# Joins of two 32-blocks at once on 64 rows, a schedule that counts instructions in lots of 256, and the fourth unit inverted in larger blocks on the vector engine

## The chip, the cores and the metric

One core of one Trainium2 chip. The time is the device time of one launch in microseconds (us); a run is one execution, and a kernel is judged by the median of its runs and by its ratio to the kernel before on the same chip.

## The reference, cut to what matters

```python
# deltanet: q, k, v of (4, 8, 768, 48), beta of (4, 8, 768)
for t in range(S):                       # 768 steps
    y[:, :, t] = einsum('bhd,bhde->bhe', q[:, :, t], state)
    v_old = einsum('bhde,bhd->bhe', state, k_n[:, :, t])
    state = state + beta * einsum('bhd,bhe->bhde', k_n[:, :, t], v[:, :, t] - v_old)
# mixer on x = y as (4, 768, 384)
u = x + (x^T U V)^T
out = u + relu(u @ w_ch1) @ w_ch2
```

The kernel turns the 768 steps into 12 chunks of 64. Each chunk and head needs the inverse of a 64x64 unit triangular matrix. A "unit" is half a batch: 6 chunks of all 8 heads. There are eight units. A batch's recurrence needs its two units inverted; its mixer then gives TensorE 288 large matmul passes (128x128 by 384 columns, `p_f` and `p_o`; a *pass* is one matmul instruction as the profile counts it, and a call in the program makes two: the 384 calls of `p_e` are 768 passes in the kernel before), which also fill TensorE's gaps in other batches' stages.

## The kernel before

Inversion starts on VectorE on small diagonal blocks: the 48 heads and chunks of a unit have two diagonal blocks of 32x32 each, 96 blocks on 96 partitions. Units 0 to 3 do this in 16x16 blocks (`split = 2`, 15 steps of two VectorE instructions). Two *joins* on TensorE then make 32x32 and 64x64 inverses of them. Units 4 to 7 do it in 32x32 blocks (`split = 1`, 31 steps), and only the second join is left. Joins run in thirds of a unit. The first join, `p_e` and `p_d`, is what the change rewrites:

```python
split = 2 if n < 4 else 1                # n: the unit
...
quarter = [slice(BK * i, BK * i + BK) for i in range(4)]      # BK = 32
p_e = ps_of([128, TQ, SB], "p_e")                             # TQ = 8, SB = 16
for e, (c, j, r) in enumerate(where):                         # 8 slots of two heads and chunks
    for i, rows in enumerate(quarter):                        # four calls each
        at = slice(BK * (i % 2), BK * (i % 2) + BK)
        nc.tensor.matmul(p_e[rows, e], pg[rows, c, j, r, at], zc[rows, e, SB:BK], ...)
...
turned(zn, zc)                                                # VectorE transposes
nc.scalar.mul(xe, p_e, mask_e)
...
for e in range(TQ):
    for rows in quarter:
        nc.tensor.matmul(p_d[rows, e], zn[rows, e], xe[rows, e], ...)
```

A small scheduler in the kernel's Python orders all work. Each `step(pe=, dve=, act=, ...)` gives an estimated duration per engine, and the work that could start first is emitted next. Each engine's queue is filled in that order.

The first stage of a unit runs thus: Gram matrices `pg` to memory (`scr`), back as `gs`, then ScalarE takes the keys' norms from its diagonal (`nc.scalar.sqrt(norm, gs...)`), then VectorE inverts.

## Time and profile before

| | before |
|---|---|
| time, 4 runs | 673.27 us median (671.5 to 675.08) |
| span of the profiled run | 672.2 us |
| first pass of `p_e`; last but one right side of the first batch made | 41.73; 112.6 us |
| first batch's front (`p_tt`), first large pass `p_f` | 120.6; 130.47 us |
| unit 2's joins | 152.14 to 179.12 us |
| last pass of TensorE | 668.8 us |

A *right side* is the VectorE subtraction `rhs` with which each chunk of the recurrence begins (eleven of a batch). The *front* is the mixer's start, which waits for the recurrence's end. The profile's lines are shown in the prediction.

### The profile page before, as it was taken

Reading aid. Unit: us, or ns where it says so; the run is one execution under the profiler, and the core shown is the slowest. Engines: PE = TensorE matmul, PEld = TensorE weight load, DVE = VectorE, ACT = ScalarE, POOL = GpSimd, SP = SyncE. Lnnn points to the kernel's source line nnn. Section 1 sums busy time; section 2 is a strip of 40 time slices with the busy share of each in tenths; the row PEclk is TensorE's granted clock in tenths of the full one; section 3 lists DMA queues with packets and bytes.
Section 4 is the critical chain, followed back from the end, with each engine's and each line's share of the span. In section 5 each row is a group of like instructions: output and inputs, shape, how many; then the busy total and the mean of one; then the engine's idle time right before and its main releaser. Section 6 shows DMA issues by size and latency. Waiting matters only on the chain.

```text
span 672.2 us, 21750 instructions
## 1 busy us (share of the span) xinstructions
PE 619.1 (92%) x9696; PEld 391.7 (58%) x9696; DVE 302.2 (45%) x739; ACT 189.4 (28%) x479; POOL 227.3 (34%) x378
## 2 busy tenths in 40 slices
PE   4468877897998999999998999999999999999997
PEld 3357766555655665555655555566565555555554
DVE  3498656994472122895861106869811112100000
ACT  3314645334501553102211331133113310310210
POOL 9653185856260393824501825530000000000000
PEclk9655555896899699999998999999999999999999
DMA  8766266665132133316212323251030000000000
GB/s 130 187 150 159 69 155 166 153 168 111 40 94 51 38 74 80 77 39 139 39 45 57 88 41 73 61 112 32 14 72 14 2 14 13 12 1 23 12 13 23
DMA packets 83566, 47.73 MB, mean 71 GB/s; under 512 B 71984, under 2 KB 76640, under 8 KB 83472
## 3 DMA queue, kind: packets, MB, share of 16 engines
q0 software_dynamic: 14528, 26.98, 17.0%
q1 hardware_dynamic: 64208, 18.66, 12.6%
q8 instruction: 76, 1.25, 0.8%
q10 hardware_dynamic: 4736, 0.69, 0.6%
q14 instruction: 18, 0.15, 0.1%
HBM read 35.29 MB, written 11.01 MB: 69 GB/s over the span
## 4 chain that ended last, share of the span: by engine, by line
PE 87%; DVE 4%; DMA 3%; issue 3%; ACT 2%; SPq 0%; ACTq 0%; DVEq 0%
PE p_f L1057 31%; PE p_o L1078 29%; PE p_y L889 5%; PE p_g L542 4%; PE p_s L923 3%; PE p_s L937 3%; PE p_y L945 2%; PE p_d L824 2%; PE p_x L844 2%; PE p_v L861 1%; PE p_e L811 1%; PE p_u L1021 1%; PE p_h L1011 1%; PE p_tt L987 1%; DVE xt L691 1%
## 5 line engine op out<-in xcount | busy, mean ns | idle before, releaser
L1057 PE MATMUL p_f<-ut,w_sb 128*128 128x384 f32 x576 | 213.3, 515 | 0.0
L1078 PE MATMUL p_o<-w_sb,h_f 128*128 128x384 f32 x576 | 203.1, 497 | 0.0
L1057 PEld LDWEIGHTS p_f<-ut,w_sb 128*128 128x128 f32 x576 | 107.1, 196 | 65.0 <-issue 3.9
L1078 PEld LDWEIGHTS p_o<-w_sb,h_f 128*128 128x128 f32 x576 | 104.2, 189 | 63.9 <-issue 1.2
L1039 ACT ACTIVATE h_f<-p_f 128x384 f32<-128x384 f32 x96 | 47.1, 491 | 159.0 <-PE p_f L1057 158.9
L475 POOL DMA_DIRECT2D qn<-in_k_dram x96 | 58.7, 619 | 52.8 <-DVE qt L484 43.3
L414 POOL DMA_DIRECT2D vn<-in_v_dram x64 | 41.9, 666 | 88.8 <-DVE rhs L916 81.5
L475 POOL DMA_DIRECT2D qn<-in_q_dram x96 | 58.8, 620 | 22.2 <-DVE prod L685 14.4
L1044 DVE TENSOR_TENSOR x<-x,p_o 128x384 f32<-128x384 f32 x24 | 13.2, 553 | 112.5 <-PE p_o L1078 112.3
L691 DVE TENSOR_TENSOR xt<-xt,prod 96x30 f32<-96x30 f32 (+20 forms) x184 | 56.9, 309 | 6.3
L685 DVE TENSOR_TENSOR prod<-gs,xt 96x30 f32<-96x30 f32 (+20 forms) x184 | 56.4, 306 | 5.0
L960 DVE TENSOR_TENSOR s<-s,p_s 128x192 f32<-128x192 f32 x40 | 14.1, 352 | 92.1 <-PE p_s L937 81.2
L967 ACT COPY x<-p_y 64x192 f32<-64x192 f32 x96 | 30.1, 314 | 53.8 <-PE p_y L945 50.1
L916 DVE TENSOR_TENSOR rhs<-vn,p_y 128x192 f32<-128x192 f32 x44 | 15.6, 354 | 65.4 <-PE p_y L889 64.9
L932 ACT COPY z<-p_s 128x192 f32<-128x192 f32 x48 | 15.3, 319 | 103.7 <-PE p_s L923 103.4
L414 POOL DMA_DIRECT2D kn<-in_k_dram x48 | 31.4, 663 | 6.7 <-PE p_s L937 5.8
L923 PEld LDWEIGHTS p_s<-rhs,zt 64*64 64x64 f32 x704 | 17.2, 158 | 25.9 <-issue 19.3
L923 PE MATMUL p_s<-rhs,zt 64*64 64x48 f32 x704 | 23.0, 254 | 6.5 <-DVE rhs L916 4.9
L889 PEld LDWEIGHTS p_y<-s,kt 48*64 48x64 f32 x704 | 16.7, 155 | 18.8 <-issue 10.3
L937 PEld LDWEIGHTS p_s<-z,kn 64*64 64x64 f32 x704 | 16.8, 155 | 17.2 <-issue 12.5
L945 PE MATMUL p_y<-z,qk 64*64 64x48 f32 x768 | 23.1, 242 | 0.5 <-ACT z L932 0.5
L889 PE MATMUL p_y<-s,kt 48*64 48x48 f32 x704 | 22.5, 250 | 1.0 <-ACT x L967 1.0
(132 smaller groups left out, 622.3 us busy)
## 6 DMA issues: line engine op xcount, KB each, us to landing
wide<-in_moe_w_ch_dram POOLq DMA_DIRECT2D x7, 768.0 KB, 5.6
vn<-in_v_dram POOLq DMA_DIRECT2D x64, 72.0 KB, 2.6
out_dram<-x SPq DMA_DIRECT2D x24, 192.0 KB
kn<-in_k_dram POOLq DMA_DIRECT2D x48, 72.0 KB, 2.5
gs<-scr SPq DMA_DIRECT2D x8, 384.0 KB
scr<-xt SPq DMA_DIRECT2D x8, 384.0 KB
scr<-pg SPq DMA_DIRECT2D x30, 96.0 KB
stage<-in_moe_w_ch_dram POOLq DMA_DIRECT2D x3, 768.0 KB, 5.1
```

The costliest lines, as they stand in the source:

```text
L414: engines[queue].dma_start(out=t[half(g ^ (s % 2) if crossed else g), :, s], in_=src[b, 4 * g + s, hf * UC * L : (hf + 1) * UC * L, :].rea ...
L475: nc.gpsimd.dma_start(out=places[rows, x, j, :, 0 : ds.stop - ds.start], in_=src[b, h, hf * UC * L : (hf + 1) * UC * L, ds].rearrange("(m ...
L685: nc.vector.tensor_tensor(out=prod, in0=gb[:, :, j : j + 1, j + 1 :].to_broadcast([NP, split, m, w]), in1=xb[:, :, 0:m, j : j + 1].to_broa ...
L691: nc.vector.tensor_tensor(out=xb[:, :, 0:m, j + 1 :], in0=xb[:, :, 0:m, j + 1 :], in1=prod, op=ALU.subtract,)
L889: nc.tensor.matmul(p[half(x ^ par), par, D * (2 * i + j) : D * (2 * i + j) + D], kq[i][half(par, D), x, j, cu], s_old[half(par, D), x, j], ...
L923: nc.tensor.matmul(p_s[half(x), par, D * (2 + j) : D * (2 + j) + D], zt[half(x ^ par), cu, j, par], rhs[half(x ^ par), 2 * j + par], start ...
L937: nc.tensor.matmul(p_s[half(par), x, D * j : D * j + D], kn[half(x), cu, 2 * j + par], z[half(x), 2 * j + par], start=True, stop=True,)
L945: nc.tensor.matmul(p_y[half(x ^ par), par, D * (2 + j) : D * (2 + j) + D], qk[half(x), cu, par, j], z[half(x), 2 * j + par], start=(c == 0 ...
L967: nc.scalar.copy(tokens_of(b, c, g), pair_of(p_y, 1)[half(g)])
L1039: nc.scalar.activation(hs[f], p_f, ACTF.Relu)
L1057: nc.tensor.matmul(p_f, w1_sb[:, t, f * 128 : (f + 1) * 128], ut[:, t], start=(t == 0), stop=(t == KT - 1),)
L1078: nc.tensor.matmul(p_os[c], hs[e][:, c * 128 : c * 128 + 128], w2_sb[:, e], start=(e == 0), stop=(e == FT - 1),)
```

## The change

Its intent: fewer TensorE instructions where TensorE runs out of them, and fewer small passes. That it runs out is read from the trace of the kernel before. Eight of its gaps are "issue" in the middle of a group (0.52 to 1.97 us, 11.6 us in all; *fetch stalls* from here on). Each ends 1.27 to 1.57 us after a packet of 16,384 bytes of the instruction queue has landed, and each stands 0.75 to 0.76 of a lot past a whole number of lots of 256 TensorE instructions, counted from the first.

1. Joins of units 0 to 2 take two 32-blocks per call: 64 rows by 64 columns of weights, 32 columns moved, half the calls. Work is done in place in `zt`; the copies of the diagonal blocks go, and the transposes double.
2. Unit 3 is inverted in 32x32 blocks on VectorE and loses its first join.
3. The scheduler counts instructions and puts work off that would run ahead of a lot of 256.

```diff
-        split = 2 if n < 4 else 1
+        split = 2 if n < 3 else 1
...
-        p_e = ps_of([128, TQ, SB], "p_e")
+        p_e = ps_of([128, TQ, 2, SB], "p_e")
         for e, (c, j, r) in enumerate(where):
-            for i, rows in enumerate(quarter):
-                at = slice(BK * (i % 2), BK * (i % 2) + BK)
-                nc.tensor.matmul(
-                    p_e[rows, e], pg[rows, c, j, r, at], zc[rows, e, SB:BK],
-                    start=True, stop=True,
-                )
+            for g in range(2):
+                rows = half(g)
+                nc.tensor.matmul(
+                    p_e[rows, e], pg[rows, c, j, r], odd[rows, e], start=True, stop=True
+                )
...
-        nc.scalar.mul(xe, p_e, mask_e)
+        for a in range(2):
+            nc.scalar.mul(xe[:, :, a], p_e[:, :, a], mask_e[:, a : a + 1])
...  (p_d likewise: zn[half(g), e] and xe[half(g), e])
+    LOT, FETCH = 256, 4.1
+    def fetched(at, s, goes=False):
+        left = LOT - lot["used"]
+        if s["ins"] >= left:
+            ahead = s["pe"] * clock["slow"] * left / s["ins"]
+            at = max(at, lot["since"] + FETCH - ahead)
+            if goes:
+                lot.update(since=at + ahead, used=s["ins"] - left)
+        elif goes:
+            lot["used"] += s["ins"]
+        return at
...  (cut: the clearing of zt for unit 2, renamed buffers, an "ins" count on each step)
```

More of the change, by code (lines that the diff above doesn't have):

```diff
@@ L107 @@
     clock = dict(now=0.0, at=0.0, pe=0.0, dve=2.5, act=0.8, sp=0.8, pool=3.8, slow=1.6)
+    LOT, FETCH = 256, 4.1
+    lot = dict(since=0.0, used=0)
     free = dict(pair=[0.0] * 2, one=[0.0] * 2, mix=[0.0] * 2)
@@ L113, in need, with step @@
         return [k for k in keys if all(x >= 0 for x in k[1:])]
-    def step(pe=0, dve=0, act=0, sp=0, pool=0, then=0.0, on=None, take=(), give=()):
+    def step(pe=0, dve=0, act=0, sp=0, pool=0, then=0.0, on=None, take=(), give=(), ins=64):
         return dict(
-            pe=pe, dve=dve, act=act, sp=sp, pool=pool, then=then, on=on, take=take, give=give
+            pe=pe, dve=dve, act=act, sp=sp, pool=pool, then=then, on=on, take=take, give=give, ins=ins
         )
@@ L159, in run @@
                 )
+                if s["pe"]:
+                    at = fetched(at, s)
                 could.append((at, i, engine))
@@ L178, in run @@
             if s["pe"]:
+                fetched(at, s, True)
                 ends["pe"] = clock["pe"] = at + s["pe"] * clock["slow"]
@@ L210 @@
         nc.gpsimd.memset(t[:, :, :, D:DP], 0.0)
-    mask_e = const.tile([128, 1], FP32, name="mask_e")
+    mask_e = const.tile([128, 2], FP32, name="mask_e")
     bias_e = const.tile([128, 1], FP32, name="bias_e")
     warm = const.tile([128, 1], FP32, name="warm")
-    gates = const.tile([NP, 2], FP32, name="gates")
+    gates = const.tile([128, 2], FP32, name="gates")
     quarters = const.tile([128, 4, BK], FP32, name="quarters")
@@ L234, in later_constants @@
         for i in range(4):
-            nc.gpsimd.memset(mask_e[BK * i : BK * i + BK // 2], 1.0)
+            nc.gpsimd.memset(mask_e[BK * i : BK * i + BK // 2, i % 2 : i % 2 + 1], 1.0)
         nc.gpsimd.memset(bias_e, -896.0 * 2.0 ** 7)
@@ L398, in gate @@
         yield step(pool=0.2)
-        nc.gpsimd.tensor_copy(out=gates[:, i : i + 1], in_=gated[i])
+        rows, value = gated[i]
+        nc.gpsimd.tensor_copy(out=gates[rows, i : i + 1], in_=value)
         emitted(("opened", i))
@@ L507, in turn @@
             t = ts[0][0]
-            yield step(pe=0.7 if t is qt else 0.5, then=0.1, take=("one",))
+            yield step(pe=0.7 if t is qt else 0.5, then=0.1, take=("one",), ins=8)
             p_t = ps_one([128, 2, 2, 2 * L], "p_t")
@@ L642, in norms @@
         def norms():
-            yield step(pe=0.25, then=0.1, take=("one",))
+            yield step(pe=0.25, then=0.1, take=("one",), ins=16)
             p_n = ps_one([128, CS], "p_n")
@@ L677, in blocks @@
         if n == 0:
-            gated[0] = gs[:, 0, 0:1]
+            gated[0] = slice(0, NP), gs[:, 0, 0:1]
             emitted(("gate", 0))
@@ L708, in blocks @@
             HQ = CS // 2
-            zc = single.tile([128, HQ, BK], FP32, name="zc", tag="zc")
-            zn = single.tile([128, HQ, BK], FP32, name="zn", tag="zn")
+            zc = single.tile([128, HQ, BK], FP32, name="zc", tag="xz")
+            zn = single.tile([128, HQ, BK], FP32, name="zn", bufs=2)
             for i in range(4):
@@ L721, in blocks @@
             where = [(e, x, g) for e in range(HQ) for x in range(2) for g in range(2)]
-            yield step(pe=0.95, then=0.1, take=("one",))
+            yield step(pe=0.95, then=0.1, take=("one",), ins=192)
             p_x = ps_one([128, HQ, BK], "p_x")
@@ L734, in blocks @@
             yield step(act=0.5, then=0.1, give=("one",))
-            xz = single.tile([128, HQ, BK], FP32, name="xz", tag="zc")
+            xz = single.tile([128, HQ, BK], FP32, name="xz", tag="xz")
             nc.scalar.copy(xz, p_x)
-            yield step(pe=0.95, then=0.1, take=("pair",))
+            yield step(pe=0.95, then=0.1, take=("pair",), ins=192)
             p_v = ps_pair("p_v")
@@ L758, in blocks @@
             return
-        if n != 1:
-            zc = single.tile([128, CS, BK], FP32, name="zc", tag="zc")
-            zn = single.tile([128, CS, BK], FP32, name="zn", tag="zn")
-        else:
-            zc, zn = [
-                early[:, i : i + CS * BK].rearrange("p (q t) -> p q t", q=CS) for i in (1536, 2304)
-            ]
+        yield need(("clear", n if n > 1 else -1))
         yield step(sp=1.1 if n == 0 else 2.2 if n < 2 else 3.2, act=1.1 if n == 0 else 0)
         for i in range(4):
-            two[i % 2].dma_start(out=zc[BK * i : BK * i + BK], in_=blk[i])
+            two[i % 2].dma_start(out=diagonal(zt, i), in_=blk[i])
         emitted(("compact", n), 3.2)
         for third in range(3):
-            begin(join(n, third, pg, zt, zc, zn), 2.3 + 0.1 * (3 * n + third))
+            begin(join(n, third, pg, zt), 2.3 + 0.1 * (3 * n + third))
     def diagonal(t, i):
@@ L782, in turned, with clear, join @@
         nc.vector.transpose(zn.rearrange("p q t -> p (q t)"), zc.rearrange("p q t -> p (q t)"))
-    def join(n, third, pg, zt, zc, zn):
+    def clear(n):
+        yield need(("rec", n - 2))
+        yield step(pool=1.4)
+        for g in range(2):
+            nc.gpsimd.memset(
+                zts[n % 2][L * g : L * g + BK].rearrange("p c j r t -> p (c j r) t")[:, :, BK:L],
+                0.0,
+            )
+        emitted(("clear", n))
+    def join(n, third, pg, zt):
         SB, TQ = BK // 2, CS // 3
@@ L797, in join @@
         where = [(e // 4, e // 2 % 2, e % 2) for e in range(TQ * third, TQ * third + TQ)]
-        quarter = [slice(BK * i, BK * i + BK) for i in range(4)]
-        zc, zn = zc[:, qs], zn[:, qs]
+        zq = zt.rearrange("p c j r t -> p (c j r) t")[:, qs]
+        odd = zq.rearrange("p q (a u s) -> p q a u s", a=2, u=2)[:, :, :, 1]
         yield need(("compact", n))
@@ L803, in join @@
         if (n, third) == (0, 0):
-            gated[1] = zc[0:NP, 0, 0:1]
+            gated[1] = slice(96, 128), zq[96:128, 0, BK : BK + 1]
             emitted(("gate", 1))
-        yield step(pe=0.7 if n < 2 else 0.6, dve=0.0, then=0.6 if n > 1 else 0.1, take=(bank,))
-        p_e = ps_of([128, TQ, SB], "p_e")
+        if n == 1:
+            at = 1536 + TQ * L * third
+            zn = early[:, at : at + TQ * L].rearrange("p (q t) -> p q t", q=TQ)
+        yield step(pe=0.7 if n < 2 else 0.6, dve=0.0, then=0.1, take=(bank,))
@@ L808, in join @@
+        if n != 1:
+            zn = single.tile([128, TQ, L], FP32, name="zn", bufs=2)
+        p_e = ps_of([128, TQ, 2, SB], "p_e")
         for e, (c, j, r) in enumerate(where):
-            for i, rows in enumerate(quarter):
-                at = slice(BK * (i % 2), BK * (i % 2) + BK)
+            for g in range(2):
+                rows = half(g)
                 nc.tensor.matmul(
-                    p_e[rows, e], pg[rows, c, j, r, at], zc[rows, e, SB:BK],
-                    start=True, stop=True,
-                )
@@ L816, in join @@
-        xe = room([128, TQ, SB], "xe")
-        yield step(act=0.4, dve=0.45, then=0.1, give=(bank,))
-        turned(zn, zc)
-        nc.scalar.mul(xe, p_e, mask_e)
-        yield step(pe=0.7 if n < 2 else 0.6, then=0.6 if n > 1 else 0.1, take=(bank,))
-        p_d = ps_of([128, TQ, SB], "p_d")
-        for e in range(TQ):
-            for rows in quarter:
-                nc.tensor.matmul(p_d[rows, e], zn[rows, e], xe[rows, e], start=True, stop=True)
-        yield step(dve=0.75, then=-0.35, give=(bank,))
@@ L826, in join @@
-        nc.vector.tensor_tensor(
-            out=zc[:, :, SB:BK], in0=zc[:, :, SB:BK], in1=p_d, op=ALU.subtract
-        )
-        turned(zn, zc)
-        def blocks_of_32():
-            first = (n, third) == (0, 0)
-            yield step(act=0.75, dve=0.6) if first else step(act=1.5)
-            for i in range(4):
-                copy = nc.vector.tensor_copy if first and i % 2 else nc.scalar.copy
-                copy(diagonal(zt, i)[:, qs], zc[quarter[i]])
-            emitted(("diagonal", n, third), 0.1)
@@ L839, in join @@
-        yield step(pe=0.7 if n < 2 else 0.6, then=0.6 if n > 1 else 0.1, take=(bank,))
+                    p_e[rows, e], pg[rows, c, j, r], odd[rows, e], start=True, stop=True
+                )
+        xe = room([128, TQ, 2, SB], "xe")
+        yield step(act=0.65, dve=0.75, then=0.1, give=(bank,))
+        turned(zn, zq)
+        for a in range(2):
+            nc.scalar.mul(xe[:, :, a], p_e[:, :, a], mask_e[:, a : a + 1])
+        yield step(pe=0.7 if n < 2 else 0.6, then=0.1, take=(bank,))
@@ L840, in join @@
+        p_d = ps_of([128, TQ, 2, SB], "p_d")
+        for e in range(TQ):
+            for g in range(2):
+                nc.tensor.matmul(
+                    p_d[half(g), e], zn[half(g), e], xe[half(g), e], start=True, stop=True
+                )
+        yield step(dve=1.2, then=-0.75, give=(bank,))
+        nc.vector.tensor_tensor(out=odd, in0=odd, in1=p_d, op=ALU.subtract)
+        turned(zn, zq)
+        yield step(pe=0.7 if n < 2 else 0.6, then=0.1, take=(bank,))
         p_x = ps_of([128, TQ, BK], "p_x")
@@ L846, in join @@
                     pg[rows, c, j, r, 0:BK],
-                    zc[rows, e],
+                    zq[rows, e, BK:L],
                     start=True,
@@ L854, in join @@
             nc.scalar.copy(xz[L * g : L * g + BK], p_x[L * g : L * g + BK])
-        begin(blocks_of_32(), 2.35 + 0.1 * (3 * n + third))
-        yield step(pe=0.7 if n < 2 else 0.6, then=0.6 if n > 1 else 0.1, take=(bank,))
+        yield step(pe=0.7 if n < 2 else 0.6, then=0.1, take=(bank,))
         p_v = ps_of([128, TQ, BK], "p_v")
@@ L860, in join @@
                 rows = slice(L * g, L * g + BK)
-                nc.tensor.matmul(p_v[rows, e], zn[rows, e], xz[rows, e], start=True, stop=True)
+                nc.tensor.matmul(
+                    p_v[rows, e], zn[rows, e, 0:BK], xz[rows, e], start=True, stop=True
+                )
         yield step(act=0.75, give=(bank,))
@@ L864, in join @@
             rows = slice(L * g, L * g + BK)
-            nc.scalar.mul(
-                zt[rows].rearrange("p c j r t -> p (c j r) t")[:, qs, BK:L], p_v[rows], -1.0
-            )
-        yield need(("diagonal", n, third))
+            nc.scalar.mul(zq[rows, :, BK:L], p_v[rows], -1.0)
         emitted(("below", n, third), 0.2)
@@ L918, in recur @@
                 )
-            yield step(pe=0.45 if b == 0 else 0.4, then=0.1, take=("pair",))
+            yield step(pe=0.45 if b == 0 else 0.4, then=0.1, take=("pair",), ins=32)
             p_s = ps_pair("p_s")
@@ L993, in front @@
             nc.vector.tensor_copy(out=part, in_=p_t)
-            yield step(pe=0.65, then=0.1, take=("one",))
+            yield step(pe=0.65, then=0.1, take=("one",), ins=4)
             p_t = ps_one([128, DM], "p_tt")
@@ L1004, in front @@
         ut = uts[b, i] = mix.tile([128, KT, GT], FP32, name="ut")
-        yield step(pe=0.75, then=0.1, take=("pair", "one"))
+        yield step(pe=0.75, then=0.1, take=("pair", "one"), ins=12)
         two = ps_pair("p_h")
@@ L1017, in block @@
             nc.vector.tensor_tensor(out=x[:, c], in0=x[:, c], in1=p_hs[e], op=ALU.add)
-            yield step(pe=0.35, then=0.1, take=("one",))
+            yield step(pe=0.35, then=0.1, take=("one",), ins=6)
             p_u = ps_one([128, KT, 128], "p_u")
@@ L1053, in wide @@
                 if (b, i) == (0, 1) or t == 0:
-                    yield step(pe=0.65 if (b, i) == (0, 1) else 1.95, take=("mix",) if t == 0 else ())
+                    yield step(
+                        pe=0.65 if (b, i) == (0, 1) else 1.95, ins=4 if (b, i) == (0, 1) else 12,
+                        take=("mix",) if t == 0 else (),
+                    )
                 if t == 0:
@@ L1074, in wide @@
                         if e == f:
-                            yield step(pe=1.95, take=("mix",) if e == 0 else ())
+                            yield step(pe=1.95, take=("mix",) if e == 0 else (), ins=12)
                         if e == 0:
@@ L1105 @@
         order += [(wide(b, 0), 6 + b), (wide(b, 1), 6.5 + b)]
+    order += [(clear(n), 3 + 0.01 * n) for n in range(2, 3)]
     with tc.manual_schedule():
```

## The prediction

> **What bounds the kernel now.** I read the page's busy rows first, then the stretches by stage, then the chain of work that ended last, in order of time, in the stretches where TensorE is not full, and last the groups with shapes kept apart.
>
> From the page: busy time per engine, TensorE's busy tenths and granted clock in 40 slices of 16.8 us, and the instruction queue.
>
> ```profile
> PE 619.1 (92%) x9696; PEld 391.7 (58%) x9696; DVE 302.2 (45%) x739; ACT 189.4 (28%) x479; POOL 227.3 (34%) x378
> PE   4468877897998999999998999999999999999997
> PEclk9655555896899699999998999999999999999999
> q8 instruction: 76, 1.25, 0.8%
> ```
>
> TensorE is the bound from about 121 us on; before that, the first batch's recurrence runs at half clock. 9,696 passes, each with its weight load, are 19,392 instructions, and 19,392 / 256 = 75.75: the 76 packets of the instruction queue (1.25 MB / 76 = 16 KB) are TensorE's own program, 256 instructions each. A matmul call here is two passes, so four instructions.
>
> The stretches: busy time of PE, PEld, DVE, ACT and POOL, clock, DMA share, GB/s.
>
> ```profile
> 40.00:121.00 81.00, 64.43 (x2245) 57.20 (x2243) 59.34 (x127) 40.08 (x105) 42.11 (x67) 0.50 0.54 130
> 152.00:180.00 28.00, 23.46 (x763) 16.53 (x754) 10.74 (x23) 14.78 (x41) 10.01 (x16) 0.76 0.38 81
> 180.00:210.00 30.00, 29.97 (x372) 17.21 (x372) 17.67 (x52) 4.11 (x13) 15.34 (x25) 1.00 0.36 81
> 210.00:240.00 30.00, 27.61 (x811) 18.86 (x810) 6.61 (x15) 14.19 (x39) 9.96 (x16) 0.77 0.17 43
> 240.00:266.00 26.00, 26.00 (x554) 15.26 (x553) 3.54 (x10) 10.53 (x31) 13.88 (x23) 1.00 0.34 69
> ```
>
> The joins of units 0 and 1 lie in the first row, of unit 2 in the second, of unit 3 in the fourth. Only those rows have idle TensorE time and a clock under 1; the rows between are full.
>
> The chain (start, us, what) in unit 3's joins, and at a later place:
>
> ```profile
> 212.45 0.41 PE p_d L824 x34
> 212.87 1.85 issue
> 214.72 0.48 PE p_d L824 x30
> 217.36 1.58 PE p_f L1057 x2
> 235.31 0.84 PE p_f L1057 x2
> ...
> 363.40 0.95 PE p_x L727 x66
> 364.35 0.49 PE p_y L889 x24
> 364.85 1.81 issue
> 366.66 0.47 PE p_y L889 x5
> 367.12 4.14 PE p_f L1057 x6
> ```
>
> "issue" in the middle of a group that waits for no engine is TensorE without instructions. Such gaps of 0.5 to 2 us stand at 62.8, 83.3, 88.8, 103.1, 154.2, 158.6, 212.9 and 364.8 us. Counted in the trace they lie almost whole lots of 256 instructions apart, and each ends about 1.4 us after an instruction packet landed. Where lots follow closest, the packets start 3.4 us apart (70.15, 73.63, 77.00); after a stall the next lot took 4.1 us (155.9 to 160.0) and once 6.1. I take 3.5 to 4.1 us as what a lot costs at least. The second loss is the clock: the record is at half from 157.7 to 167.9, 171.4 to 174.8, 215.7 to 229.4 and 365.9 to 372.7 us, so two passes of p_f took 1.58 instead of 0.84.
>
> [...] The half-clock stretches last 3.4, 6.8, 10.2 and 13.6 us[...].
>
> **The pace of the two kinds of join.** Groups with shapes apart:
>
> ```profile
> L824 PE MATMUL p_d<-xe,zn 32*32 32x16 f32 x576 | 8.6, 195 | 7.1 <-issue 4.6 <-ACT xe L819 2.4 <-DVE zn L782 0.2
> L811 PE MATMUL p_e<-zc,pg 32*32 32x16 f32 x576 | 8.0, 191 | 0.5 <-DMA zc<-scr 0.5
> L889 PE MATMUL p_y<-s,kt 48*64 48x48 f32 x704 | 22.5, 250 | 1.0 <-ACT x L967 1.0
> L727 PE MATMUL p_x<-zt,pg 32*32 32x32 f32 x384 | 4.1, 193 | 0.0
> ```
>
> In the chain at half clock 64 passes of p_e or p_d take 0.98 us (15 ns each, over four row groups: 61 ns per row group), and 32 passes of p_y on 64 rows take 1.08 (34 ns, two row groups: 67). At full clock p_y takes 0.61 us for 32 passes, 19 ns. So a pass costs its row group about the same whatever its size. The new p_e and p_d have half the passes on half as many row groups: about 1.0 us at half clock and 0.62 at full. **The array gains next to nothing; what halves is the instructions.** The old pair of groups needs 256 instructions in 1.96 us of array time, under a lot's 3.5 to 4.1, so it starves; the new one needs 128 in 2.0.
>
> **The change, part by part.**
>
> *Instructions.* Units 0 to 2 have nine thirds; each loses 64 passes (p_e and p_d: 128 to 64). Unit 3 goes from 576 passes to 192. That is 9 x 64 + 384 = 960 passes, 1,920 instructions, 7.5 lots: 69 packets should be left.
>
> *Units 0 and 1 (40 to 121 us).* TensorE's 64.4 us of passes stay. Its idle time is 16.6 us, of which 1.11 + 1.34 + 1.97 + 0.52 = 4.9 is fetch; by the built order every lot in this stage now holds about 4.2 us of half-clock work, so this goes. ScalarE loses four copies of 0.40 us per third and gains one scaled copy of 0.37: it frees a wait of 1.5 us at 67.6. VectorE pays: the transposes cover 512 columns instead of 256 (0.445 us each, about 0.85 then, two per third) and the subtraction doubles (0.29, about 0.43): some 0.9 us per third, 5 us in six, on an engine busy 59 of 81 us that also makes the recurrence's right sides. Net: **-5 us**.
>
> *Unit 2 (152 to 180).* The chain from 151.6 to 179.1 holds 12 passes of p_f (4.3 us at full clock) and 0.6 of recurrence; the other 22.7 us are joins, three Gram products, stalls, and 3.7 us of p_f at half clock. After: 480 small passes in a row are 3.75 lots, at 4.1 us 15.4, plus about 1.7 of p_f at half clock and a wait or so, 17.7. **-5 us**; the block stays fetch-bound and still drops the clock.
>
> *Unit 3 (210 to 240).* Join pieces in the chain sum to 11.9 us (the 1.85 stall included) and the excess of p_f, p_s and p_y at half clock to 4.3. In their place come two groups of 96 passes on the existing path, 0.95 us each as at 321.5 and 325.2. 16.2 - 1.9 = **-14 us**. The longer inversion, 62 VectorE instructions instead of 30 (about 22 against 8.5 us), lies where VectorE is busy 18 of 30 and 7 of 30 us.
>
> *Lots in the schedule.* Later stages keep their work. The scheduler now puts big matmuls where a lot would run dry; the 364.8 stall with its half clock (1.81 + 2.0 + 0.45, and small ones) should go: **-4 us**. Its count starts at zero while the trace's boundaries are off by some 100 instructions, so a stall elsewhere is possible.
>
> *What is given back.* Unit 3 ready later means that the first batch's mixer is eaten as filler: in the built order none is left when the second batch's recurrence ends. Its last chunk waits bare for z, s, the right side and the copies (about 2.6 us by the 0.5 to 0.7 us gaps at 107 to 120), the front then for about 1, and the clock may drop over p_tt (1.4 us, as at 120.7 against 430.6). **+5 us**. Before, 27 us of p_o were left there.
>
> Sum: -5 - 5 - 14 - 4 + 5 = -23; 673 - 23 = **650 us**.
>
> **The rivals.**
> 1. *The array's pace rules, fetch is a side show.* Then units 0 to 2 gain nothing, as the passes cost the same, and only unit 3 counts: -14 to -16 + 5, 662 to 664. For it: small stages at half clock, where even the old lots mostly hold 2.8 to 4.2 us. Against it: gaps at lot boundaries, with no other releaser.
> 2. *VectorE takes over.* The 5 us in the first stage delay right sides and weight conversion, and unit 3's inversion comes late[...]: 660 to 668. For it: 73% busy in 40 to 121. Against it: 20 us of p_f stand between chunk 5 and unit 3's blocks in the new order.
> 3. *The clock holds too.* [...]another 3 to 8 us go: 642 to 647.
>
> **Range and chances.** Unit 3's 14 us I trust within 3. The other terms, 5 us each, may each be off by their own size, partly together; that is some 8 us around 650, with the second rival's tail a little longer: 640 to 661. Two per cent is 13.5 us, 659.6. Rival 1 alone or a late inversion would bring it above. Faster 0.87, within 2% 0.12, slower 0.01.
>
> **What would show it.** 69 instruction packets; p_e and p_d at 64*64 with 288 passes each but no more than 20% less time per group at half clock; no issue gaps over 1 us before 121 us; no half clock and no dip around unit 3; gaps of 0.5 us each and perhaps half clock ahead of the second p_tt; a front row of 40 to 121 shortened by some 5 us. It is wrong if the first stage does not shorten though its fetch gaps are gone (then the pace of passes or VectorE bound it), if unit 3's p_x waits for its DMA, or if the clock loss merely moves.

## More of the kernel before

By the *tile* of a call this document means its input's partitions (rows) together with its output's partitions (columns); the profile prints the size of both ahead of the shapes, as 32*32. Old `p_e` and `p_d` thus use the four 32x32 tiles on the diagonal. The recurrence's calls (`p_y`, `p_s`) go over all four 64x64 tiles, since their list of heads pairs each row half with each column half:

```python
QUADS = ((0, 0), (1, 1), (1, 0), (0, 1))
heads = [(j, par, g) for j in range(2) for par, g in QUADS]
for j, par, x in heads:
    nc.tensor.matmul(p[half(x ^ par), par, ...], kq[i][half(par, D), x, j, cu], s_old[half(par, D), x, j], ...)
```

## The result, and the profile after

The changed kernel took 665.16 us (664.08 to 668.75, 4 runs) beside 673.27 of the kernel before: a ratio of 0.9889 with a 95% interval of 0.9843 to 0.9934. That is within 2%. A ratio is the mean time of one kernel's runs over that of the other's in the same rounds, so it is not quite the ratio of the medians. On another chip later (run e13) it was 0.9927, so the gain is about 1%, where 3.4% had been predicted.

The page of the changed kernel: busy times, TensorE's tenths and clock in 40 slices of 16.6 us, and the instruction queue.

```profile
PE 614.9 (93%) x8736; PEld 395.9 (60%) x8736; DVE 317.5 (48%) x761; ACT 169.8 (26%) x430; POOL 228.9 (35%) x380
PE   4659997698999999989999999999999999999997
PEclk9655555697599999999999999999999999999999
q8 instruction: 69, 1.13, 0.7%
```

960 passes are gone and 69 packets are left, as predicted, yet TensorE's busy time fell by 4.2 us only. From 179.0 to 663.7 us the clock's record is at 1.00.

The stretches (busy time of PE, PEld, DVE, ACT, POOL; clock, DMA share, GB/s):

```profile
40.00:121.00 81.00, 67.54 (x1792) 62.68 (x1792) 62.45 (x130) 31.87 (x87) 43.76 (x70) 0.50 0.56 137
152.00:180.00 28.00, 25.77 (x514) 20.65 (x513) 10.94 (x16) 10.86 (x29) 11.67 (x18) 0.63 0.33 69
210.00:240.00 30.00, 30.00 (x359) 17.38 (x357) 14.99 (x40) 8.29 (x22) 17.79 (x28) 1.00 0.50 104
283.00:300.00 17.00, 13.89 (x349) 8.74 (x342) 8.26 (x17) 6.41 (x18) 13.82 (x21) 1.00 0.92 177
```

Against the rows of before: in the first stage TensorE is busy *longer* with 453 passes fewer. Unit 3's stretch is full at full clock, where it had been 27.61 of 30 at 0.77. The second batch's front has 3.1 us of bare gaps, which the prediction had put in.

The groups that replaced the old joins in the changed kernel:

```profile
L842 PE MATMUL p_e<-zt,pg 64*64 64x32 f32 x288 | 16.2, 275 | 1.0 <-DMA zt<-scr 1.0
L855 PE MATMUL p_d<-xe,zn 64*64 64x32 f32 x192 | 11.0, 279 | 1.5 <-ACT xe L850 1.5
L855 PE MATMUL p_d<-xe,w_sb 64*64 64x32 f32 x96 | 5.8, 291 | 0.0
```

The waits for "issue" in front of `p_d` are gone. But 576 passes now take 33.0 us (16.2 + 11.0 + 5.8), where the 1,536 old ones of four units took 23.6. One group in the timeline, first of the kernel before, then of the changed one (start, length, engine, line, what, passes):

```profile
71.78 1.20 PE L811 MATMUL p_e<-w_sb,pg 32*32 32x16 f32 x64
80.83 1.05 PE L811 MATMUL p_e<-w_sb,pg 32*32 32x16 f32 x64
```

```profile
69.55 1.82 PE L842 MATMUL p_e<-zt,pg 64*64 64x32 f32 x30
71.13 0.34 PE L842 MATMUL p_e<-zt,pg 64*64 64x32 f32 x2
```

A length runs to the recorded end of the last pass, and one new pass by itself is recorded as 0.277 to 0.292 us long here, so the pace is read from start to start: 30 passes in the 1.58 us between 69.55 and 71.13, 53 ns apart; the 64 old ones of an undisturbed group start 13.3 ns apart. From first start to last end the new group takes 1.92 us (69.55 to 71.47) and the old one 1.05. The prediction had put both at about 1.0.

A second surprise is at 115 us. TensorE, then ScalarE, of the changed kernel:

```profile
114.71 0.68 PE L943 MATMUL p_s<-rhs,zt 64*64 64x48 f32 x16 [0.48 <-DVE rhs L936]
119.14 0.68 PE L957 MATMUL p_s<-z,kn 64*64 64x48 f32 x16 [3.74 <-ACT z L952]
```

```profile
113.10 0.94 ACT L370 ACTIVATE power<-power,bias_e 128x768 uint16<-128x768 uint16 x1
118.48 0.26 ACT L652 ACTIVATE norm<-gs 96x32 f32<-96x32 f32 x1 [4.44 <-DMA gs<-scr]
118.77 0.32 ACT L952 COPY z<-p_s 128x192 f32<-128x192 f32 x1
```

ScalarE's copy `z` was ready to start at about 115.4. Unit 2's `norm` stood ahead of it in ScalarE's queue and waited for a DMA until 118.48.

The milestones, counted from the first pass of `p_e`. That pass came at 41.73 us before and 43.49 after; ahead of it in the chain stands a DMA of the Gram matrices that took 4.89 and 7.04 us. This part of the difference is not taken for one of the change: in the traces of all runs the pass comes at 41.7 to 45.6 us with the old joins and at 42.2 to 44.9 with the new. Unit 2's end is corrected to the same amount of large passes done (the changed kernel has done 54 there and the one before 78; 24 x 0.335 us = 8.0 are added).

| from first `p_e` to | before | after | predicted change | measured |
|---|---|---|---|---|
| last but one right side | 70.9 | 70.8 | | -0.1 |
| first large pass | 88.7 | 92.2 | -5 | +3.4 |
| end of unit 2's joins | 137.4 | 138.1 | -10 | +0.7 |
| from there to the end | 489.7 | 477.1 | -13 | -12.6 |

These are single traces. The same changed kernel, traced again on another chip (e13), gave 72.1, 96.1, 144.2 and 477.0. So the first three rows can move by up to 6 us from trace to trace, and smaller differences in them are not shown; the last row is steady.

So the second half came as predicted, and the first half gave nothing that stands out of this spread. The missing 11 us are in the stages with the joins of units 0 to 2.

### The profile page after: what moved, and what is told of

Same layout as the page of the kernel before. It is cut to its first block, busy times and chain, and to the rows that moved or that the text cites.

```text
span 662.4 us, 19841 instructions
## 1 busy us (share of the span) xinstructions
PE 614.9 (93%) x8736; PEld 395.9 (60%) x8736; DVE 317.5 (48%) x761; ACT 169.8 (26%) x430; POOL 228.9 (35%) x380
## 4 chain that ended last, share of the span: by engine, by line
PE 85%; DMA 5%; DVE 4%; POOL 2%; issue 2%; ACT 1%; SPq 0%; ACTq 0%; DVEq 0%; POOLq 0%
PE p_f L1080 30%; PE p_o L1101 30%; PE p_y L909 4%; PE p_g L561 3%; PE p_s L943 3%; PE p_s L957 2%; PE p_e L842 2%; PE p_d L855 2%; PE p_y L965 2%; PE p_v L882 1%; PE p_h L1031 1%; PE p_u L1041 1%; DMA scr<-pg 1%; PE p_x L866 1%; POOL qn L494 1%
## 5 line engine op out<-in xcount | busy, mean ns | idle before, releaser
L1080 PE MATMUL p_f<-ut,w_sb 128*128 128x384 f32 x576 | 204.3, 500 | 0.0
L1080 PEld LDWEIGHTS p_f<-ut,w_sb 128*128 128x128 f32 x576 | 105.3, 191 | 64.8 <-issue 1.2
L710 DVE TENSOR_TENSOR xt<-xt,prod 96x112 f32<-96x112 f32 (+21 forms) x200 | 63.7, 319 | 6.9
L704 DVE TENSOR_TENSOR prod<-gs,xt 96x112 f32<-96x112 f32 (+21 forms) x200 | 63.2, 316 | 5.2
L952 ACT COPY z<-p_s 128x192 f32<-128x192 f32 x48 | 15.3, 319 | 94.3 <-PE p_s L943 94.0
L936 DVE TENSOR_TENSOR rhs<-vn,p_y 128x192 f32<-128x192 f32 x44 | 15.4, 350 | 42.8 <-PE p_y L909 42.5
L957 PE MATMUL p_s<-z,kn 64*64 64x48 f32 x704 | 23.0, 247 | 5.2 <-ACT z L952 5.2
```

The lines of the kernel that those rows point to most:

```text
L704: nc.vector.tensor_tensor(out=prod, in0=gb[:, :, j : j + 1, j + 1 :].to_broadcast([NP, split, m, w]), in1=xb[:, :, 0:m, j : j + 1].to_broa ...
L710: nc.vector.tensor_tensor(out=xb[:, :, 0:m, j + 1 :], in0=xb[:, :, 0:m, j + 1 :], in1=prod, op=ALU.subtract,)
L957: nc.tensor.matmul(p_s[half(par), x, D * j : D * j + D], kn[half(x), cu, 2 * j + par], z[half(x), 2 * j + par], start=True, stop=True,)
L1080: nc.tensor.matmul(p_f, w1_sb[:, t, f * 128 : (f + 1) * 128], ut[:, t], start=(t == 0), stop=(t == KT - 1),)
```

## The experiments

**Theory A**: a pass costs its *tile* the loading of its weight columns. The new groups use only two tiles (the diagonal ones), with 64 columns each, so the array time doubles and eats what the fetch stalls gave. **The prediction's theory**: a pass costs its row group the same whatever its size, so the first half must have been lost to something else. Further suspects: the norm's wait, VectorE, the schedule.

### e1: the same joins in tiles of 32 columns

```diff
             for g in range(2):
                 rows = half(g)
-                nc.tensor.matmul(
-                    p_e[rows, e], pg[rows, c, j, r], odd[rows, e], ...)
+                for u in range(2):
+                    at = slice(BK * u, BK * u + BK)
+                    nc.tensor.matmul(
+                        p_e[L * g + BK * u : L * g + BK * u + BK, e], pg[rows, c, j, r, at],
+                        odd[rows, e], ...)
...  (p_d likewise)
```

> The changed kernel with each call of p_e and p_d split into two of 32 columns, order of all else kept; results right. It has again 64 passes and 128 instructions per group, now on four array tiles of 64 rows x 32 columns instead of two of 64 x 64. Theory A (a pass costs its own tile the load of its columns, so two 64-column tiles give 120/2 = 60 ns at half clock, and four 32-column tiles some 61/4 = 15): where instructions do not run dry a group takes about 1.0 us instead of 1.93; 1.5 us or more where lots of 256 run dry, with gaps at lot boundaries again; total near 660 to 668. Theory B (a pass on 64 rows costs about 60 ns whatever its columns): the groups take 3.8 us, total near 685. Theory C (the recorded 1.93 us is really starvation by instructions): a group with twice the instructions takes about 3.8 us too, but with packets every 3.5 to 4 us.

Measured: correct, 664.19 us (660.23 to 665.14), ratio 0.9872 (0.9797 to 0.9947). Two groups in its timeline:

```profile
69.12 1.06 PE L844 MATMUL p_e<-zt,pg 64*32 64x32 f32 x60 [2.24 <-DMA beta<-in_beta_dram]
71.15 1.06 PE L844 MATMUL p_e<-zt,pg 64*32 64x32 f32 x60
73.60 0.32 PE L844 MATMUL p_e<-zt,pg 64*32 64x32 f32 x4 [1.39 <-issue]
```

Twice the passes, on the same 64 rows and moving the same 32 columns, take half the time: 13.3 ns from start to start. But with the instructions doubled the fetch stalls are back (1.39 us of "issue" ahead of the last four passes), and the first front came at 124.4 us as in the changed kernel (124.7). Before 121 us four stalls over 0.45 us stand in e1's trace, 4.4 us in all, where the changed kernel's has none in its whole span. That is about what e9, below, shows of the saved array time to reach this stage's milestones (4.6 us). Array time and fetch stalls changed places, and the stage kept its length.

### e2: half of the moved columns

```diff
-                    p_e[rows, e], pg[rows, c, j, r], odd[rows, e], ...
+                    p_e[rows, e, 0], pg[rows, c, j, r], odd[rows, e, 0], ...
...  (p_d likewise; the readers take the one half twice)
```

> The changed kernel with p_e and p_d computed for one of the two 16-column halves only and the other taken from it: wrong results on purpose, same instructions, order and stationary tiles, half the moving columns. Theory A (the load of 64 columns sets the pace): p_e and p_d stay at 1.85 to 1.95 us per 32 passes at half clock, total within 1.5 us of the changed kernel. If the moving columns set it, about 1.0 to 1.5 us per group and a total 5 to 12 us lower.

Measured: 664.68 us (664.57 to 664.83), ratio 0.9892 (0.9837 to 0.9947). Its output is wrong, which doesn't matter for the time. The weight loads in e2, then in e1:

```profile
L842 PEld LDWEIGHTS p_e<-zt,pg 64*64 64x64 f32 x288 | 15.4, 203 | 1.3 <-DMA zt<-scr 0.6 <-issue 0.5
```

```profile
L844 PEld LDWEIGHTS p_e<-zt,pg 64*32 64x32 f32 x576 | 8.3, 140 | 6.2 <-DMA beta<-in_beta_dram 2.3 <-issue 2.1 <-DMA zt<-scr 1.3
```

Moving 16 columns instead of 32 saves nothing: the loads take 15.4 us in either case, and a group of 32 passes 1.89 us where it had taken 1.92. The number of weight columns per tile sets the pace: with 32 instead of 64 on the same rows (e1) the starts are 13.3 ns apart over four tiles instead of 52.6 over two. e1 and e2 together show theory A.

With this the passes can be counted per tile at half clock. Start to start, old `p_e` takes 13.3 ns over four tiles of 32 columns, so 53 ns per tile; e1 the same. `p_x` takes 26.6 ns over two tiles of 32 columns: 53 again. New `p_e`: 52.6 ns over two tiles of 64 columns, 105 per tile. `p_s` and the `p_y` on 48 rows: 25 to 26 ns over *four* tiles of 64 columns, 100 to 103 per tile (the `p_y` on 64 rows is a little faster, 22.7 ns, 91 per tile). One count fits them to within a sixth, some 53 ns for each 32 columns loaded into a tile at half clock, and the old kernel's trace could have given it. At full clock the same count gives 35 ns per tile for 32 columns (old `p_e` 8.7 ns over four tiles, the 96 passes of unit 3's `p_x` the same) and 58 to 61 for 64 (new `p_e` 29.1 over two, `p_s` 15.3 over four).

### e3: unit 3 alone, and e4: with the lots

```diff
-        split = 2 if n < 4 else 1            # the kernel before
+        split = 2 if n < 3 else 1            # e3; e4 adds the counting of lots
```

> The kernel before with one edit, unit 3 in 32 x 32 blocks on VectorE; old joins for units 0 to 2, old scheduler. My reckoning: unit 3 gives 14 us, the bare front of the second batch takes back about 4 and the fetch stall at 365 us may stay: ratio to before 0.981 to 0.990 (660 to 667 us). If the new joins of units 0 to 2 cost net time, this alone is as fast as the whole change or faster; if they gain, it is slower than 665 by what they gain.

> As e3 plus the scheduler that counts lots, with 128 instructions given for the old p_e and p_d: the whole change without its new joins. If the new joins lose (pace of 60 ns a pass, 12 groups x 0.95 us in units 0 and 1 and 6 in unit 2, against fetch stalls of about 5 and 3 us saved): 655 to 663 us, 2 to 10 us under the changed kernel. If the new joins gain net: 667 to 672.

Measured: e3 665.0 us (662.94 to 668.48), ratio 0.9902 (0.9838 to 0.9965); e4 667.36 (666.11 to 669.4), ratio 0.9934 (0.9876 to 0.9993). One line of the change gives as much as the whole change. Counting lots on top of it gains nothing. e4's 667.36 lies where its expectation had put a net gain of the new joins (667 to 672), but without lots the joins add only the step from 0.9902 (e3) to 0.9874 (e6, below), which is within the noise. Unit 3's blocks in the changed kernel's timeline show why this part works:

```profile
240.07 1.02 PE L746 MATMUL p_x<-zt,pg 32*32 32x32 f32 x96
241.02 1.56 PE L1080 MATMUL p_f<-ut,w_sb 128*128 128x384 f32 x4
242.51 1.20 PE L760 MATMUL p_v<-xz,zn 32*32 32x32 f32 x96
```

Two groups of 96 passes stand among large passes, with no idle time and no loss of clock (its record is at 1.00 throughout the stretch 240 to 266 us).

### e5: the norm behind the recurrence

```diff
-        yield need(("inverted", n - 1), ("beta", n))
+        yield need(("inverted", n - 1), ("beta", n), ("rec", 1 if n == 2 else -1))
```

> The changed kernel, with unit 2's first stage held back until the first batch's recurrence is done, so that ScalarE's norm of unit 2 stands behind the last z and not before it. Theory A (the first stage lost its gain because that norm waited 4.4 us for its DMA at the head of ScalarE's in-order queue, and the chain z, s, right side waited behind it, TensorE idle 3.7 us at 115 us): the 3.7 us gap is gone, the last right side of the first batch comes at 118 to 119 us instead of 122.5, the first front at about 121, and the time falls by 3.5 to 5 us, to 660 to 662. Rival B (VectorE or GpSimd hold the chain in that stage and the norm wait is only the place where it shows): another wait takes the gap's place and the time stays within 1 us of the changed kernel. Rival C (unit 2 is now started too late): the time is saved at 115 us and lost again at unit 2's joins, which start later than 155 us.

Measured: correct, 668.38 us (665.45 to 670.49), ratio 0.9935 (0.9888 to 0.9983): no gain over the changed kernel, and the saving that theory A forecast did not come. The wait itself went: the last right side came at 118.3 us instead of 122.5, the first front at 120.6 instead of 124.7. But the chain then ran into the weights. In e5's chain of work:

```profile
114.42 7.45 DMA w_sb<-in_moe_w_ch_dram
...
123.98 0.88 DVE power L385
...
125.76 1.78 DVE qt L503
...
127.68 1.13 PE p_g L561 x32
```

VectorE's conversion of that weight piece could not start before the DMA landed (at 121.87 us; its first step starts at 121.96), the transposes of unit 2's queries stood behind it, and TensorE waited 1.99 us for them. The half clock lasted until 141.8 us instead of 127.8, and the first large pass came at 138.89 instead of 135.65. In the changed kernel too these transposes start at 125.76 us. So 4.1 us were saved at the front and more than that lost by the first large pass; unit 2's joins began at 159.49 us. That is the rivals B and C of this run, a bit of each.

### e6: no counting of lots, e7: the joins alone, e8: the lots alone

```diff
-    LOT, FETCH = 256, 4.1
+    LOT, FETCH = 1 << 30, 4.1       # e6; e7 as well, with the new joins on units 0 to 3:
-        split = 2 if n < 3 else 1
+        split = 2 if n < 4 else 1   # e7, which clears zt for unit 3 too
```

e8 is the kernel before with the `fetched` of the diff above and the right counts on each step.

> The changed kernel with a lot so large that the scheduler never counts one to its end: both new forms of joins and the 32x32 blocks of unit 3, ordered as the kernel before was. If the counting is worth what the prediction said (4 us) this takes about 669; if it is worth next to nothing, as the run with unit 3 and lots against the one with unit 3 alone suggests, it stays at 664 to 666. Issue gaps of 1 to 2 us in the middle of pass groups should come back at some places outside the joins (before: 1.8 us at 365 us).

> The 64-row joins on all four units (unit 3 as well, so no unit in 32x32 blocks on VectorE) and no counting of lots. Theory A (a diagonal pair of 64-column tiles takes 60 ns a pass at half clock, so a group of 32 passes costs 1.9 us and the 64 old passes cost 1.0 us; fetch stalls saved and array time lost cancel): 671 to 676, the same as before. The prediction's theory (32 passes cost what 64 did): 12 thirds without stalls, 10 to 13 us less, 660 to 663.

> The kernel before, with the scheduler that counts instructions in lots (the old joins counted with 128 passes' instructions each group) and nothing else changed. The prediction's theory (the 1.8 us stall at 365 us and its half clock go): 669. If counting is worth nothing, as the other pair suggests: 672 to 675; the stall at 365 us may then be gone and another be there in its place.

| | us, median (range) | ratio to before |
|---|---|---|
| e6, the change without lots | 663.83 (663.35 to 665.04) | 0.9874 (0.9833 to 0.9915) |
| e7, the new joins alone | 675.79 (672.52 to 680.85) | 1.0055 (0.9988 to 1.0122) |
| e8, the lots alone | 679.36 (676.9 to 684.76) | 1.0112 (1.005 to 1.0175) |

e7 is what theory A said: the joins by themselves are worth nothing, where the prediction's theory gave 660 to 663. Counting lots is worth nothing in the changed kernel (e6) and costs 1.1% by itself (e8), which neither theory had said. The stall it was meant to remove, at 365 us, was absent in e6 as well, whose trace has no fetch gap over 0.45 us at all (its expectation had them come back), so it went with the other parts of the change. In e8 stalls of 1.7 to 2.0 us stood at other places, once in the middle of the large passes that had been moved there to prevent it. e8's timeline:

```profile
164.49 1.88 PE L1078 MATMUL p_f<-ut,w_sb 128*128 128x384 f32 x5
168.06 1.13 PE L1078 MATMUL p_f<-ut,w_sb 128*128 128x384 f32 x3 [1.69 <-issue]
```

### e9 and e12: the prediction's assumption made true

If the array time of the new groups is what ate the gain, then groups that cost 1.0 us must bring the predicted time. Half of the passes do that: `p_e` and `p_d` for every other head, whose neighbours read the same block. All other instructions stay (VectorE's subtraction is split in two). The groups' instructions are halved along with their array time; but as the changed kernel's trace has no fetch gap over 0.45 us, there was none for that to remove. e12 is the changed kernel with this; e9 has e5's later norm too. Their outputs are wrong, which doesn't matter for the times.

```diff
-        p_e = ps_of([128, TQ, 2, SB], "p_e")
-        for e, (c, j, r) in enumerate(where):
+        p_e = ps_of([128, TQ // 2, 2, SB], "p_e")
+        for e, (c, j, r) in list(enumerate(where))[::2]:
...  (p_d likewise; the readers take each block twice)
```

> Wrong result on purpose. The run with the later norm, with p_e and p_d of the new joins computed for every other head only (16 passes of a group instead of 32, the readers take the neighbour's block): each group should take about 0.97 us at half clock instead of 1.93 and hold 64 instructions, so it has neither the array time of the new form nor the starving of the old one. Theory A (array time is what the new form spends where the old one starved): the right side of the last chunk but one of the first batch, at 114.2 us with all passes, comes 8 to 11 us earlier, at 103 to 106. Rival B (VectorE, GpSimd or the weights' conversion set the pace of that stage, array time and stalls lie beside them): it comes at 111 to 114. Should TensorE's time go but the front not follow, the weights' conversion holds the front, as it did with the later norm.

> Wrong result on purpose. The changed kernel itself with p_e and p_d for every other head only, the norm left where it is. This is the world the prediction assumed: new groups of about 1.0 us at half clock. If the array time of the new groups is what lost the gain, the last right side but one of the first batch comes at 109 to 110 us as in the run with the later norm, and the time is 652 to 657, where the prediction said 650. If the norm's wait at 115 us takes back what is saved, the first front stays at 122 to 125 us and the time at 658 to 664.

> The changed kernel on the same chip: 664 to 666 as before, for the comparison with the two others of this call.

Measured: e9 654.74 us (652.59 to 656.44), ratio 0.9766 (0.9718 to 0.9813). e12 655.75 (653.09 to 658.32), ratio 0.9729 (0.967 to 0.9787); the changed kernel on the same chip (e13) 669.18 (667.39 to 670.82), ratio 0.9927 (0.9882 to 0.9971). e13 itself came above its expected 664 to 666. So 13.4 us lie between e13 and e12. The array time taken away is 12 groups x 0.85 us (1.92 - 1.07) in units 0 and 1 and 4.4 us in unit 2 (six groups of 8.9 us in the changed kernel's trace, of 4.6 in e12's; half of them ran at full clock), 14.6 us. 673 x 0.9729 = 655, inside the predicted range of 640 to 661.

A group of e12 in the timeline, at the assumed cost:

```profile
76.39 1.07 PE L859 MATMUL p_d<-xe,w_sb 64*64 64x32 f32 x16
```

The milestones of e12, in the form of the table above, against before: last but one right side 66.0 (-4.9), first large pass 85.7 (-3.1), end of unit 2's joins 127.6 (-9.8, predicted -10), from there to the end 477.6 (-12.1, predicted -13). In this trace the stage terms come out near the predicted ones once the group costs what it was assumed to cost. Against e13's trace, on the same chip, the first three are -6.1, -10.4 and -16.6; so the gain is shown, and its split over the stages only to within several us. (The right side came at 110.8 us, where 109 to 110 had been expected.)

e9's last but one right side came at 109.6 us, between what theory A (103 to 106) and its rival (111 to 114) had said: of 12 x 0.85 = 10.2 us of array time taken from that stage, 4.6 reached this milestone (against e5's 114.2). The rest lay beside other waits. So TensorE is not the only bound there, and rival B holds for the other part.

### e10, e11 and e14: unit 2 on VectorE too

```diff
-        split = 2 if n < 4 else 1            # the kernel before
+        split = 2 if n < 2 else 1            # e10 and e14; e11: the same in the changed kernel
```

> The kernel before with units 2 and 3 both in 32x32 blocks on VectorE, old joins for units 0 and 1, old scheduler. Unit 3 alone gave 8 us of time. If leaving work out of TensorE is what pays: unit 2's joins go too, some 12 to 16 us of TensorE's time at half clock, less what its longer inversion (22 instead of 8.5 us on VectorE, where it converts weights) holds back: 650 to 660. If the inversion comes too late for the second batch (its recurrence starts at 183 us), TensorE waits bare for it and the time is 662 or more.

> The changed kernel with unit 2 also in 32x32 blocks on VectorE: new joins for units 0 and 1, lots counted. As the new joins and the lots have each come out at nothing or worse, this should be within 5 us of the run with old joins for units 0 and 1, and 5 to 12 us under the changed kernel if unit 2's inversion is in time.

> The kernel with units 2 and 3 in 32x32 blocks, old joins and old scheduler, on the same chip: 659 to 661, so 4 to 6 us under the changed kernel, if the earlier difference of 3 to 5 us between runs of different calls was one of the kernels and not of the chips.

| | us, median (range) | ratio to before |
|---|---|---|
| e10 | 660.23 (659.15 to 660.46) | 0.9855 (0.9819 to 0.9892) |
| e11 | 663.5 (660.19 to 665.46) | 0.9902 (0.9856 to 0.9949) |
| e14, e10 again, beside e13 | 664.23 (662.25 to 665.76) | 0.9852 (0.9805 to 0.9899) |

e11 was expected 5 to 12 us under the changed kernel and is level with it (0.9902 against 0.9889 and 0.9927). e14 was expected at 659 to 661 us; it missed that, but is 5 us under e13, as expected.

The old joins and the old schedule with both units on VectorE have the lowest ratio of the correct versions (e6's interval overlaps with theirs): on one chip 664.23 beside 669.18 of the changed kernel, 0.9852 / 0.9927 = 0.992 of it, and the same ratio to before on two chips. It gains less than the 12 to 16 us of joins that it leaves out, because unit 2's inversion, 135.7 to 160.4 us in e10's chain, is late and TensorE waits on what comes after it (in e10's chain, also a DMA of weights of 4.99 us ahead of the transposes `qt`):

```profile
171.67 1.16 PE L542 MATMUL p_g<-qt,kt 48*64 48x64 f32 x64 [2.62 <-DVE qt L484]
173.57 1.13 PE L542 MATMUL p_g<-qt,kt 48*64 48x64 f32 x32 [0.74 <-DVE qk L558]
174.64 1.48 PE L727 MATMUL p_x<-zt,pg 32*32 32x32 f32 x90
177.10 0.33 PE L727 MATMUL p_x<-zt,pg 32*32 32x32 f32 x6 [0.98 <-issue]
```

## Why the prediction was wrong, point by point

- **The pace of the two kinds of join: the failed step.** "So a pass costs its row group about the same whatever its size", and from it "about 1.0 us at half clock" for a new group. It measured 1.92. The fit was made on `p_e` (four tiles) and `p_y`. The 67 ns "per row group" of `p_y` were two tiles of 64 columns working at the same time in that row group (26 ns from start to start over four tiles, 103 per tile); the new groups have only one tile in each (52.6 over two, 105 per tile). The row-group count fitted the old groups and was out by nearly two for the new ones. e1 and e2 show that columns loaded per tile set the pace, and e12 that with 1.0-us groups the time lies in the predicted range.
- **Units 0 and 1, -5.** The fetch gaps went, as said. In their place came 12 groups x 0.87 (1.92 - 1.05) = 10.4 us of array time. At the last but one right side the two kernels are level (-0.1). The +3.4 at the first large pass is there at the last right side already (79.0 against 75.6 us), and between the two right sides lies the norm's wait, 3.7 us that the prediction did not see. That the wait made the +3.4 is not shown: e5 took it away, and the first large pass came later still, behind the weights' conversion. VectorE's extra work, which the second rival feared, is in e12 as well, and there the stage gained 4.9 at the same milestone, so it was not what took the whole gain.
- **Unit 2, -5.** Between the first large pass and its end the changed kernel gained 2.7 (+0.7 less +3.4). The six groups took 8.9 us where the old ones took 4.6, so 4.3 us of array time were not in the sum; in e12, without them, the same stretch gained 6.7 (-9.8 less -3.1). The term was also misread: the chain from 151.6 to 179.1 holds six passes of `p_o` as well (2.13 us at 176.37), which the 22.7 us counts with the joins. Without them the same sum gives about -3.
- **Unit 3, -14, the lots, -4, and +5 given back: the sum right.** From unit 2's end on -12.6 us instead of -13. But without lots (e6) the same part takes 476.9 us, and with them 477.1, so the lots' -4 was wrong, and unit 3 with what it gives back is worth about -12.6 by this ledger instead of -9 (in e3's trace, with unit 3 alone, the stretch is 479.2 us, -10.5). Two errors cancel, so that the sum fits is luck. By the timed runs unit 3 alone gives 1.0% (e3).
- **The rivals.** The first said 662 to 664, "Then units 0 to 2 gain nothing, as the passes cost the same, and only unit 3 counts". Its time was nearest, and its reading of what counts was right. Its reason was not: fetch was no side show: in e1 the array time goes, the stalls come back, and the time stays. It shared a chance of 0.12 with the second rival, which was too little for what rested on one fit of the pace.
- **Signs named in advance.** "It is wrong if the first stage does not shorten though its fetch gaps are gone (then the pace of passes or VectorE bound it)": this is what happened, and it was the pace.

What stays open: how the 10 us of array time in the first stage split between VectorE, the DMAs and the weights' conversion once TensorE is relieved, as only 4.6 of them reached the recurrence; and why counting lots by itself costs 1.1%.

## What to carry to other kernels

Judge a small matmul by the tile that it occupies, columns loaded times passes over tiles in use, before you join two calls into a larger one: here halving the calls nearly doubled the time of a group (1.05 to 1.92 us), because two tiles of 64 columns lay where four of 32 had. Fewer instructions and less array time can stand in for one another (in e1 4.4 us of fetch stalls came in the place of array time worth some 4.6), so test each with the other held, as with the half-passes run. And try the simplest part of a change alone: one line gave all of this one's gain.

## What the traces showed besides

- Passes on different column tiles of the same rows run beside one another. In e1 the calls of one row group go to two column tiles, and 64 passes on two row groups start 13.3 ns apart, as fast as those on four row groups before. Their weight loads overlap: the 576 of `p_e` in e1 are 140 ns long each in the record and cover 8.3 us together.
- The recorded starts of matmuls do not always follow the program. In the changed kernel's timeline two passes of `p_s` start at 90.11 us, ahead of the last two of a group of `p_e` at 90.19, which stands before them in the program.
- The clock's record can be incomplete. e10's clock row starts with full clock up to 172 us (1.00 in its stretch 40 to 120), while 64 passes of `p_e` at 80.87 us took the 0.98 us that the same group takes at 80.90 us in the kernel before, where the record is at 0.50. Check the record against the pace of a known group.

```profile
PEclk9999999999789999999999999999999999999999
```
